# A linear-attention and two-layer-pair kernel: a third place for output copies, a shorter norm chain, ordered gram loads and new planner constants

## The chip, the cores and the metric

The kernel runs on one NeuronCore of a Trainium2 chip. The metric is the device time of one execution in microseconds (us); lower is better. TensorE (PE) has two clock levels, 1.2 and 2.4 GHz; the profile gives the granted share (0.5 or 1.0).

## The reference

```python
k_n = k / (norm(k) + 1e-6)                      # 4 batches x 8 heads, 768 tokens, 48 features
for t in range(768):                            # delta rule, state 48x48 per head
    y[t]   = q[t] @ state
    v_old  = state^T @ k_n[t]
    state += beta[t] * outer(k_n[t], v[t] - v_old)
x = y as [3072 tokens, 384]
x = elu(x @ w_in1) @ w_out1                     # first network, 384 -> 2048 -> 384
h = x @ w_in2                                   # second network
g = (a0 + a1 h + a2 h^2 + a3 h^3) / (1 + |b0||h| + |b1| h^2 + 1e-6)
out = g @ w_out2
```

## The kernel before, in words

**Numbers.** All is fp32. Each wide product is made of three fp32r matmuls on a high and a low part of both operands (high x high, high x low, low x high). The raw weights are taken apart bit by bit on the chip (`conv_load`, `conv_x`, `conv_d`, `conv_s`: a load of 192 KB, two ACT operations on it, one on DVE, and a split).

**Stages.** The 768 tokens are 12 subchunks of 64, two to a window, so there are 6 windows of 512 token columns. The attention of a window is: gram matrices of k with k and q (`g_item`, tile `gp`; 32 matmuls, which the trace shows as 64 MATMUL rows, because each plain fp32 matmul is two of them), the inversion of triangular matrices for all its heads (`t_pieces`, DVE with some ACT), then per subchunk the chain `ks`, `so` (tile `cb`), `lo`, `so`, `yy` (tile `y`), `xx` (transposes, tile `xt`) and `ku` in small matmuls. The first network of a window follows one window behind: for each of 16 blocks of hidden features nine matmuls into `h` (`H`), the elu on ACT and DVE (`A1`, `B1`, `C1`), nine matmuls into three accumulators `o` (`O`). After the 16 blocks `evac1` copies the three accumulators on ACT to tiles `xe` and stores each to `x2d` in DRAM. The second network reads `x2d` back and works on pairs of blocks (tiles `h_a`, `h_b`, `o`). "F" is the planner's name for the wide groups of nine matmuls.

**Order.** Nothing runs when it is recorded. `Recorder` collects all operations with their data dependences, and `order` plans them: `simulate` is a list scheduler on the host with a model of each engine, of the DMA bus and of instruction fetch for PE, and `backward` gives due times. It is run eight times, one run for each entry of `PUSH`; the plan with the earliest simulated end is the one that is emitted. Ties are moved by pseudo-random numbers (`draw`, `mixed`) whose seeds are in `MIX`. Any other seed or constant is therefore another order of the instructions on every engine's queue, of the DMA issues on SP too. Each queue runs in order.

**The planner's fetch model.** In `issue` and `stall` (lines 457 to 479) a counter adds up PE instructions, 2 for a matmul of the groups F and xx and 4 for others. The instructions come in blocks of some 254. A block is asked for when the counter gets within `room` of what is there, `wait` ns after that, at least `space` ns after the last request, and not before the modelled DMA bus is free; it can be used 2450 ns later. Where a small group would wait longer than `hold` for instructions, the planner takes a wide group first.

**Gram inputs.** `gin_ahead` loads k and q for the gram products, two halves (`hf` 0 and 1) of 512 KB for each subchunk. The first six halves have tiles of their own at the start; the other 18 go to two tiles `gin`. `g_item` asks for the next two halves at once, as soon as both tiles are free. `hold(t)` writes one element of a tile on POOL from another tile, so that the load into it waits for that. `follow`, in the change, uses the same means.

**Start.** `start` issues the first gram loads at once. Up to the first wide group PE has little to do; `gaps` puts unused matmuls (line 1501, tile `fill`, 512 columns each, two MATMUL rows per matmul) into the idle time that the plan shows.

**Norms.** For each window `pre1` gets the squared norms x of the keys and rr = x^-0.5 by Ln and Exp on ACT. `pre2` refines the norm on DVE (u = rr x, and a Newton step to t1), adds 1e-6, takes the reciprocal, squares it with a minus sign and multiplies with beta. The result scales the gram matrices before the inversion; t1, transposed to `n_t`, scales the values (`prep`, POOL).

Of the kernel before, what the change touches and what calls it, by code (L numbers as in the profile page):

```python
# [179 lines left out]
class Recorder:  # L180
# [129 lines left out]

PEC = {
    "F": (226.7, 425), "gp": (29, 475), "ks": (22, 330), "so": (22, 220), "lo": (22, 250), "yy": (31, 262), "ku": (47, 263),
    "xx": (90, 405), "wm": (200, 500), "yt": (33, 260)}
LEAVE = {"F": 2040, "so": 774, "lo": 812, "ks": 1500, "gp": 1086, "ku": 855, "yy": 1079, "xx": 290, "wm": 500, "yt": 1400}
ENTER = {"F": 0, "so": 71, "ks": 71, "xx": -25, "ku": 70, "yy": 20, "gp": 60, "lo": 100, "wm": 50, "yt": 20}
PAIR = {
# [3 lines left out]
SIZE = {"F": 9, "yy": 32, "yt": 48}  # L320
SLACK = {"small": 150, "F": 100, "x": 30, "issue": 450, "rate": 385, "land": 2300, "wait": 1500, "space": 3900, "room": 290, "first": 432, "hold": 400, "jit": 300,  "pj": 0}
MIX = [
    (44833516, 1), (87665163, 200), (70946401, 60), (44846256, 60), (55763056, 60),
]


PUSH = [(2000, 3000), (10000, 3000), (9000, 3000), (9000, 3000), (17000, 3000), (23000, 3000), (16000, 3000), (21000, 3000)]


def draw(seed, n):  # L330
# [71 lines left out]
def simulate(ops):  # L402
# [54 lines left out]
    def issue(u, t, k):  # L457
        nonlocal count, asked, shift
        shift = 0.0
        q = 2 if u.kind in ("F", "xx") else 4  # L460
        for o in u.ops:
            t0 = t + o.off * k + shift
            count += q
            if count > SLACK["first"] - SLACK["room"] + 254.6 * len(usable):
                asked = max(t0 + SLACK["wait"], asked + SLACK["space"], bus)
                usable.append(asked + 2450)
            if count > SLACK["first"] + 254.6 * used[0]:
                shift += max(0.0, usable[used[0]] - t0)
                t0 = max(t0, usable[used[0]])
                used[0] += 1  # L470
            o.start = t0

    def stall(u, t):
        n = len(u.ops) * (2 if u.kind in ("F", "xx") else 4)
        i = SLACK["first"] + 254.6 * used[0] - count
        if n < i:
            return 0.0
        a = usable[used[0]] if len(usable) > used[0] else max(t + SLACK["wait"], asked + SLACK["space"], bus) + 2450
        return a - t - max(0.0, i) / n * (u.ops[-1].off + u.ops[-1].pitch)

    def choose(e, t):
# [18 lines left out]
    while done < total:  # L500
        pick = None
        for e in free:
            if pend[e] or head[e]:
                t = free[e] if head[e] else max(free[e], pend[e][0][0])
                if pick is None or t < pick[0]:
                    pick = t, e
        t, e = pick
        while pend[e] and pend[e][0][0] <= t:
            _, n, u = heapq.heappop(pend[e])
            head[e].append((u.rank if e == "PE" else u.late, n, u))  # L510
        if e == "PE":
            small = [x for x in head[e] if x[2].kind != "F"] if mode not in (None, "F") else None
            x = min(small or head[e])
            if x[2].kind != "F" and SLACK["hold"] and stall(x[2], t) > SLACK["hold"]:
                wide = [y for y in head[e] if y[2].kind == "F"]
                if wide:
                    x = min(wide)
            head[e].remove(x)
            u = x[2]
            if mode is not None:  # L520
                stop = began + pe_cost(mode, u.kind) * size
                t = max(t, stop)
                clock(began, t if fill else stop, t)
                if fill and t > max(stop, 20000) + 500:
                    i = int((t - max(stop, 20000) - 300) / 430)
                    count += 4 * (i // 2 + i % 2)
                    while count > SLACK["first"] - SLACK["room"] + 254.6 * len(usable):
                        asked = max(t - 3000, asked + SLACK["space"], min(bus, t))
                        usable.append(asked + 2450)
                    while count > SLACK["first"] + 254.6 * used[0]:  # L530
                        used[0] += 1
            fill = fill and u.kind != "F"
            mode, began = u.kind, t
            k = 2.0 if slow else 1.0
            size = k * len(u.ops) / SIZE[mode] if mode in SIZE else k
            issue(u, t, k)
            began = t = t + shift
            free[e] = t + (u.ops[-1].off + u.ops[-1].pitch) * .95 * k
            for o in u.ops:
                finish(o, o.start + o.lat + 70 * (k - 1))  # L540
        else:
            o = choose(e, t)
            if o is None:
                free[e] = pend[e][0][0]
                continue
            o.start = t
            if e == "SP":
                if len(landed) >= 8:
                    t = o.start = max(t, landed[-8])
                free[e] = t + o.pitch  # L550
                bus = max(bus, t + 300) + o.bytes / SLACK["rate"]
                landed.append(max(t + o.lat, bus + SLACK["land"]))
                finish(o, landed[-1])
            else:
                if o.port:
                    t += max(0.0, port - t - 135)
                    port = t + o.lat
                free[e] = t + o.pitch
                finish(o, t + o.lat)
        done += 1  # L560
# [28 lines left out]
def kernel(  # L589
# [90 lines left out]
    def hold(t):  # L680
        gpsimd.tensor_copy(out=t[:, 0, 0:1], in_=gate[-1])

    conv_q = []
    for f in range(NF):
        conv_q += [("i1", f, h) for h in range(2)]
# [87 lines left out]
    def gin_ahead(n):  # L773
        for _ in range(n):
            i = gin_n[0]
            if i == len(gin_q) or i >= 4 and len(gate) < 2:
                return
            park = i < 6
            if park or gin_l[0] < 2:
                w, s, hf = gin_q[i]  # L780
                if park:
                    t = gin_park(i)
                else:
                    t = ap2.tile([128, 1024], F32, tag="gin", name="gin", bufs=2)
                    gin_l[0] += 1
                t = t.rearrange("p (u n) -> p u n", u=8)
                if 4 <= i < 8:
                    hold(t)
                rc.dma(out=t, in_=c_kg[s, hf])
                gin_t[s, hf] = t, not park  # L790
                gin_n[0] += 1
# [73 lines left out]
    def t_pieces(w):  # L865
# [17 lines left out]

        def pre2():
            v = vector
            x, rr, dg = st["x"], st["rr"], st["dg"]
            t1, u = small("t1"), small("nb")
            v.tensor_tensor(out=u, in0=rr, in1=x, op=ALU.mult)
            v.scalar_tensor_tensor(out=t1, in0=u, scalar=-0.5, in1=rr, op0=ALU.mult, op1=ALU.mult)
            v.scalar_tensor_tensor(out=t1, in0=t1, scalar=1.5, in1=u, op0=ALU.add, op1=ALU.mult)  # L890
            v.tensor_scalar(out=t1, in0=t1, scalar1=1e-6, scalar2=None, op0=ALU.add)
            v.reciprocal(out=rr, in_=t1)
            v.scalar_tensor_tensor(out=x, in0=rr, scalar=-1.0, in1=rr, op0=ALU.mult, op1=ALU.mult)
            v.tensor_tensor(out=x, in0=x, in1=bl_t.pop(w), op=ALU.mult)
            a = diag(am_f, 4)[:, :, :, 0:4]
            v.tensor_tensor(
                out=a, in0=a, in1=x.rearrange("p (d a) -> p d a", a=4).unsqueeze(3).to_broadcast([128, 8, 4, 4]), op=ALU.mult)
            v.tensor_scalar(
                out=tt_f[:, 0:132].rearrange("p (c x) -> p c x", x=33)[:, :, 0:32].rearrange("p c (b k) -> p c b k", k=4)[:, :, :, 0],
                in0=x.rearrange("p (b c) -> p c b", c=4), scalar1=-1.0, scalar2=None, op0=ALU.mult)  # L900
            for n in (4, 8):
                act(out=gs[n], in_=diag(am_f, 2 * n)[:, :, n:2 * n, 0:n], func=AF.Copy)
            gpsimd.memset(am[:, 0:16, 16:32], 0.0)
            n_t = ap2.tile([128, 32], F32, tag="n_t", name="n_t")
            n_d[w] = n_t
            v.transpose(out=n_t, in_=t1)
# [294 lines left out]
    def evac1(w):  # L1201
        NC = 256 * len(WINS[w])
        c0 = 256 * WINS[w][0]
        for c in range(3):
            if w == NW - 1:
                xs = p2q.tile([128, 512], F32, tag="ys", name="xe", bufs=3)[:, 0:NC]
            else:
                xs = mp.tile([128, 512], F32, tag="xe", name="xe")[:, 0:NC]
            act(out=xs, in_=acc[w][c][:, 0:NC], func=AF.Copy)
            rc.dma(out=x2d[:, c, c0:c0 + NC], in_=xs)  # L1210
        del acc[w]
# [141 lines left out]
            c += d  # L1353

    def start():
        gin_ahead(1)
        rc.dma(out=cm_sb, in_=mask_p)
        gin_ahead(3)
        load_beta(0)
# [227 lines left out]
```

## Time and profile before

| | |
|---|---|
| runs shown | 1003.8, 1006.26, 995.06 us; median 1003.8 |
| the profiled execution | 1006.48 us, span 1004.7 us |
| PE busy | 979.2 us, 97% |
| DVE, ACT, POOL busy | 819.8 us (82%), 692.6 us (69%), 311.7 us (31%) |
| share of the critical chain | PE 88%, DMA 4%, DVE 3%, ACT 2% |
| q1 data, q8 instruction packets | 59408 of 98.30 MB, 86 of 1.41 MB |

A busy PE is not a PE at its peak: matmuls overlap, and their ends are modelled. The chain of waits is followed back from the last instruction; "issue" in it is time in which an engine waited for nothing that the profile shows. In the rows, "[1.91 <-issue]" is idle time of the engine just before the instruction and what ended it.

### The profile page before, as it was taken

The page shows a single profiled execution, that of the slowest core. Times are in us where ns is not written, and L with a number is a line of the kernel's source. Part 1 is how long each engine was busy: PE and PEld are TensorE (multiplying, and loading weights), DVE is VectorE, ACT ScalarE, POOL GpSimd, SP SyncE. Part 2 cuts the span into 40 slices and gives each one's busy share as a digit, 9 for nine tenths or more (in the row PEclk, how much of TensorE's full clock was granted, in tenths as well). Part 3 has the DMA queues.
Part 4 walks back from the last instruction along what each step waited for, and adds up shares of the span by engine and source line. Part 5 has one row for each costly group of instructions (what it writes and reads, how often), then busy time and mean ns, then how long its engine had stood idle before and what let it go on. Part 6 is the DMA issues. An engine that isn't in the chain of part 4 may idle for free.

```text
span 1004.7 us, 26301 instructions
## 1 busy us (share of the span) xinstructions
PE 979.2 (97%) x11038; PEld 779.0 (78%) x11038; DVE 819.8 (82%) x1164; ACT 692.6 (69%) x1330; POOL 311.7 (31%) x218
## 2 busy tenths in 40 slices
PE   7989989999999999999999999999999999999997
PEld 4557777877787787788877888888888888888885
DVE  4998868956896996799543467999999999999997
ACT  4287878776867887686755577677676767766764
POOL 2000000432221231222112234363473644633341
PEclk9999999999999999999999999999999999999999
DMA  8352564146517543641505732001010010000000
GB/s 273 144 157 80 172 210 123 57 125 224 176 36 237 167 136 101 219 132 64 177 18 191 296 95 79 1 2 62 1 63 1 1 63 1 32 1 1 32 1 31
DMA packets 59526, 99.97 MB, mean 100 GB/s; under 512 B 6544, under 2 KB 39440, under 8 KB 59408
## 3 DMA queue, kind: packets, MB, share of 16 engines
q1 hardware_dynamic: 59408, 98.30, 30.1%
q8 instruction: 86, 1.41, 0.6%
q14 instruction: 32, 0.26, 0.1%
HBM read 76.25 MB, written 22.02 MB: 98 GB/s over the span
## 4 chain that ended last, share of the span: by engine, by line
PE 88%; DMA 4%; DVE 3%; ACT 2%; issue 2%; SPq 0%; ACTq 0%; DVEq 0%
PE o L198 37%; PE h L198 19%; PE h_b L198 10%; PE h_a L198 9%; PE cb L198 3%; PE fill L1501 3%; PE gp L198 2%; PE y L198 2%; PE ks L198 2%; DMA o2d<-cs 1%; PE ku L198 1%; DMA raw<-w_out 1%; DMA x2d<-xe 1%; PE h_c L198 1%; DVE wo L198 1%
## 5 line engine op out<-in xcount | busy, mean ns | idle before, releaser
L198 POOL TENSOR_TENSOR gl<-wo 128x1024 fp32r<-128x1024 f32 x47 | 145.8, 3103 | 200.2 <-DVE wo L198 134.5
L198 PE MATMUL o<-gh,wor 128*128 128x512 f32 x576 | 198.5, 401 | 1.9 <-ACT xe L198 1.9
L198 PE MATMUL h<-xh,wi 128*128 128x512 f32 x546 | 189.9, 405 | 0.0
L198 ACT ACTIVATE wo<-wo 128x1024 f32<-128x1024 f32 (+3 forms) x202 | 134.9, 698 | 59.5 <-DVE wo L198 54.2
L198 POOL TENSOR_TENSOR wor<-wo,wor 128x384 fp32r<-128x384 f32 x80 | 89.2, 1116 | 249.7 <-ACT wor L198 236.6
L198 PE MATMUL o<-gh,wo 128*128 128x512 f32 x576 | 138.5, 389 | 0.0
L198 PEld LDWEIGHTS o<-gh,wor 128*128 128x128 f32 x576 | 109.6, 190 | 27.1 <-ACT xe L198 2.3
L198 PEld LDWEIGHTS o<-gh,wo 128*128 128x128 f32 x576 | 108.1, 188 | 22.5
L198 PEld LDWEIGHTS h<-xh,wi 128*128 128x128 f32 x546 | 103.8, 190 | 24.5 <-issue 0.8
L198 PE MATMUL o<-gl,wor 128*128 128x512 f32 x288 | 113.7, 395 | 0.0
L198 DVE TENSOR_TENSOR gl<-e,gh 128x512 fp32r<-128x512 f32 x88 | 73.5, 835 | 42.3 <-ACT gh L198 40.4
L198 PE MATMUL h<-xl,wi 128*128 128x512 f32 x273 | 107.8, 395 | 0.0
L198 DVE SCALAR_TENSOR_TENSOR e<-e,h 128x512 f32<-128x512 f32 x91 | 62.1, 683 | 45.6 <-ACT e L198 45.2
L198 PE MATMUL h_b<-xh,wi 128*128 128x512 f32 x300 | 96.4, 389 | 0.0
L198 PE MATMUL h_a<-xh,wi 128*128 128x512 f32 x276 | 88.9, 389 | 0.0
L198 DVE SCALAR_TENSOR_TENSOR wo<-wo 128x1024 f32<-128x1024 f32 (+2 forms) x71 | 81.8, 1160 | 7.3 <-ACT wo L198 7.1
L198 ACT ACTIVATE e<-h 128x512 f32<-128x512 f32 x91 | 54.0, 593 | 48.4 <-PE h L198 48.1
L198 ACT ACTIVATE gh<-e 128x512 fp32r<-128x512 f32 x96 | 60.0, 625 | 25.9 <-DVE e L198 16.8
L198 PE MATMUL o<-gl,wo 128*128 128x512 f32 x288 | 73.5, 390 | 2.0 <-DVE gl L198 2.0
L198 DVE SCALAR_TENSOR_TENSOR gh<-wo,ab_sb 128x1024 fp32r<-128x1024 f32 (+1 forms) x49 | 63.6, 1297 | 8.8 <-ACT wo L198 3.2
L198 POOL TENSOR_TENSOR kv<-kv,n_t 128x384 f32<-128x384 f32 x24 | 23.1, 963 | 152.1 <-PE xt L198 67.0
L198 ACT ACTIVATE wo<-h_b,ab_sb 128x1024 f32<-128x1024 f32 (+1 forms) x52 | 57.0, 1127 | 18.2 <-PE h_b L198 18.2
(148 smaller groups left out, 1876.3 us busy)
## 6 DMA issues: line engine op xcount, KB each, us to landing
kq<-c_kq SPq DMA_DIRECT2D x22, 512.0 KB, 5.3
kv<-c_kv SPq DMA_DIRECT2D x24, 384.0 KB, 4.5
gin<-c_kg SPq DMA_DIRECT2D x18, 512.0 KB, 5.3
raw<-w_out SPq DMA_DIRECT2D x42, 192.0 KB, 3.5
raw<-w_in SPq DMA_DIRECT2D x34, 192.0 KB, 3.0
o2d<-cs SPq DMA_DIRECT2D x32, 192.0 KB, 3.4
i2d<-cs SPq DMA_DIRECT2D x32, 192.0 KB, 3.3
wi<-i2d SPq DMA_DIRECT2D x16, 384.0 KB, 3.5
```

What stands on the lines that cost most here:

```text
L198: fn(**{k: v.real() if isinstance(v, View) else v for k, v in kw.items()})
L1501: nc.tensor.matmul(out=wt["w"][:, 0:256 * n].rearrange("p (a b) -> p a b", a=n), lhsT=c[:, 128:256], rhs=c.unsqueeze(1).to_broadcast([128, ...
```

## The change

Besides other seeds and pushes for the planner, the model of instruction fetch gets other constants: blocks of 253.9 instead of 254.6, first 460 for 432, `room` 264 for 290, `wait` 900 for 1500, `space` 3500 for 3900 and 2250 for 2450 ns until a block can be used. A warm-up group "wm" of three matmuls of 512 columns stands ahead of the first loads, and its kind is counted with 2 instructions per matmul and costed at 585 ns each. `xe` gets three buffers in place of the pool's two. The second half of a gram pair from half 9 on (eight of the loads) waits by a one-element POOL copy for the landing of the first half. `pre2` takes 1/(x + 2e-6 u + 1e-12) straight away and makes t1 afterwards.

```diff
-    "xx": (90, 405), "wm": (200, 500), "yt": (33, 260)}
+    "xx": (90, 405), "wm": (585, 900), "yt": (33, 260)}
...
-SLACK = {... "wait": 1500, "space": 3900, "room": 290, "first": 432, "hold": 400, "jit": 300,  "pj": 0}
+SLACK = {... "wait": 900, "space": 3500, "room": 264, "first": 460, "blk": 253.9, "use": 2250, "hold": 400, "jit": 300,  "pj": 0}
 MIX = [
-    (44833516, 1), (87665163, 200), (70946401, 60), (44846256, 60), (55763056, 60),
+    (50701903, 1), (14530668, 200), (81070061, 60), (66735086, 60), (52417381, 200), (37322455, 600),
...
-PUSH = [(2000, 3000), (10000, 3000), (9000, 3000), (9000, 3000), (17000, 3000), (23000, 3000), (16000, 3000), (21000, 3000)]
+PUSH = [(1000, 0), (2000, 3000), (17000, 3000), (1000, 3000), (15000, 3000), (21000, 3000), (13000, 3000), (21000, 3000)]
...
-        q = 2 if u.kind in ("F", "xx") else 4
+        q = 2 if u.kind in ("F", "xx", "wm") else 4
...
+    def follow(t, u):
+        gpsimd.tensor_copy(out=t[:, 0, 0:1], in_=u[:, 0, 0:1])
...
                 if 4 <= i < 8:
                     hold(t)
+                elif i >= 8 and hf:
+                    follow(t, gin_t[s, 0][0])
                 rc.dma(out=t, in_=c_kg[s, hf])
...
+            v.tensor_scalar(out=t1, in0=x, scalar1=1e-12, scalar2=None, op0=ALU.add)
             v.tensor_tensor(out=u, in0=rr, in1=x, op=ALU.mult)
+            v.scalar_tensor_tensor(out=x, in0=u, scalar=2e-6, in1=t1, op0=ALU.mult, op1=ALU.add)
+            v.reciprocal(out=x, in_=x)
+            v.scalar_tensor_tensor(out=x, in0=x, scalar=-1.0, in1=bl_t.pop(w), op0=ALU.mult, op1=ALU.mult)
             v.scalar_tensor_tensor(out=t1, in0=u, scalar=-0.5, in1=rr, op0=ALU.mult, op1=ALU.mult)
             v.scalar_tensor_tensor(out=t1, in0=t1, scalar=1.5, in1=u, op0=ALU.add, op1=ALU.mult)
             v.tensor_scalar(out=t1, in0=t1, scalar1=1e-6, scalar2=None, op0=ALU.add)
-            v.reciprocal(out=rr, in_=t1)
-            v.scalar_tensor_tensor(out=x, in0=rr, scalar=-1.0, in1=rr, op0=ALU.mult, op1=ALU.mult)
-            v.tensor_tensor(out=x, in0=x, in1=bl_t.pop(w), op=ALU.mult)
...
-                xs = mp.tile([128, 512], F32, tag="xe", name="xe")[:, 0:NC]
+                xs = mp.tile([128, 512], F32, tag="xe", name="xe", bufs=3)[:, 0:NC]
...
     def start():
+        z = tmp[:, 0:512]
+        vector.memset(z, 0.0)
+        rc.brk("wm")
+        for _ in range(3):
+            mm(out=h_s[0], lhsT=z[:, 0:128], rhs=z, start=True, stop=True)
         gin_ahead(1)
```

## Rows read from the trace of the kernel before

**Rows 1.** Busy us by stage: PE, PEld, DVE, ACT, POOL, clock, DMA share, GB/s

```profile
50.00:81.00 31.00, 26.09 (x857) 17.34 (x854) 27.83 (x74) 27.99 (x87) 1.97 (x3) 1.00 0.56 172
81.00:550.00 469.00, 461.13 (x7575) 367.79 (x7576) 351.76 (x690) 341.51 (x848) 103.42 (x96) 0.99 0.43 136
600.00:977.00 377.00, 377.00 (x1665) 312.28 (x1664) 353.60 (x274) 260.52 (x266) 177.91 (x77) 1.00 0.07 24
```

**Rows 2.** PE's waits from 81 to 620 us: total, times, longest

```profile
PE ks L198 <- issue: 3.0, 1, 3.0
PE ks L198 <- ACT gl__2915 L198: 2.4, 1, 2.4
PE gp L198 <- issue: 1.9, 1, 1.9
PE o L198 <- ACT xe L198: 1.9, 1, 1.9
```

**Rows 3.** Chain of waits from 78 to 95 us: start, length, what

```profile
79.09 1.91 issue
...
81.44 5.93 PE h L198 x18
...
88.86 2.26 PE h L198 x9
```

**Rows 4.** Chain of waits from 135 to 150 us

```profile
139.24 2.95 issue
...
142.52 3.11 PE h L198 x9
145.63 2.79 PE o L198 x9
```

**Rows 5.** DMA from 134 to 143 us: issues, KB, us to landing

```profile
gin<-c_kg SPq DMA_DIRECT2D x2, 512.0 KB, 8.1
```

**Rows 6.** Timeline from 235 to 248 us, all engines

```profile
236.55 1.19 SPq L198 DMA_DIRECT2D gin<-c_kg  x2
...
240.69 0.36 ACT L198 ACTIVATE cs<-ce 128x192 fp32r<-128x192 f32 x1 [0.83 <-DMA o2d<-cs]
...
241.37 2.04 PE L198 MATMUL ks<-s_st,kq 48*32 48x48 f32 x128 [2.35 <-ACT gl__2915 L198]
```

**Rows 7.** Chain of waits from 236 to 252 us

```profile
243.42 3.53 PE o L198 x9
```

**Rows 8.** Chain of waits from 540 to 560 us

```profile
538.50 8.84 DMA x2d<-xe
...
549.26 3.28 PE o L198 x8
552.53 2.48 PE h L198 x9
```

**Rows 9.** The stretch after 549.9 us, columns as in rows 1

```profile
549.90:553.20 3.30, 3.30 (x10) 2.52 (x9) 1.83 (x3) 2.46 (x6) 1.01 (x1) 0.50 1.03 400
```

**Rows 10.** Chain of waits from the start

```profile
5.88 1.74 PE gp L198 x54
...
9.57 2.81 PE gp L198 x95
...
12.78 1.22 PE gp L198 x33
...
26.20 1.09 PE gp L198 x64
```

**Rows 11.** Weight loads of the unused matmuls, 12 to 20 us

```profile
15.80 0.33 PEld L1501 LDWEIGHTS fill<-cm_sb 128*128 128x128 f32 x1 [0.52 <-issue]
16.65 0.33 PEld L1501 LDWEIGHTS fill<-cm_sb 128*128 128x128 f32 x1 [0.52 <-issue]
```

**Rows 12.** The norm chain's DVE operations: duration ns min/median/max

```profile
L198 DVE SCALAR_TENSOR_TENSOR t<-nb,rr x6: 183/191/193, 19.0 to 423.8; 128x32 f32<-128x32 f32 x6
```

**Rows 13.** Packets of the fetch queue from 470.9 to 474.4 us

```profile
q8 instruction: 2, 0.03, 3.6%
```

More of the change, by code (lines that the diff above doesn't have):

```diff
@@ L312 @@
     "F": (226.7, 425), "gp": (29, 475), "ks": (22, 330), "so": (22, 220), "lo": (22, 250), "yy": (31, 262), "ku": (47, 263),
-    "xx": (90, 405), "wm": (200, 500), "yt": (33, 260)}
-LEAVE = {"F": 2040, "so": 774, "lo": 812, "ks": 1500, "gp": 1086, "ku": 855, "yy": 1079, "xx": 290, "wm": 500, "yt": 1400}
+    "xx": (90, 405), "wm": (585, 900), "yt": (33, 260)}
+LEAVE = {"F": 2040, "so": 774, "lo": 812, "ks": 1500, "gp": 1086, "ku": 855, "yy": 1079, "xx": 290, "wm": 1755, "yt": 1400}
 ENTER = {"F": 0, "so": 71, "ks": 71, "xx": -25, "ku": 70, "yy": 20, "gp": 60, "lo": 100, "wm": 50, "yt": 20}
@@ L320 @@
 SIZE = {"F": 9, "yy": 32, "yt": 48}
-SLACK = {"small": 150, "F": 100, "x": 30, "issue": 450, "rate": 385, "land": 2300, "wait": 1500, "space": 3900, "room": 290, "first": 432, "hold": 400, "jit": 300,  "pj": 0}
+SLACK = {"small": 150, "F": 100, "x": 30, "issue": 450, "rate": 385, "land": 2300, "wait": 900, "space": 3500, "room": 264, "first": 460, "blk": 253.9, "use": 2250, "hold": 400, "jit": 300,  "pj": 0}
 MIX = [
-    (44833516, 1), (87665163, 200), (70946401, 60), (44846256, 60), (55763056, 60),
+    (50701903, 1), (14530668, 200), (81070061, 60), (66735086, 60), (52417381, 200), (37322455, 600),
+    (39513789, 60), (96818129, 600), (44511796, 200), (58732419, 200), (61486538, 200), (56621892, 200),
+    (59016650, 200), (65322403, 200),
 ]
-PUSH = [(2000, 3000), (10000, 3000), (9000, 3000), (9000, 3000), (17000, 3000), (23000, 3000), (16000, 3000), (21000, 3000)]
+PUSH = [(1000, 0), (2000, 3000), (17000, 3000), (1000, 3000), (15000, 3000), (21000, 3000), (13000, 3000), (21000, 3000)]
 def draw(seed, n):
@@ L463, in issue @@
             count += q
-            if count > SLACK["first"] - SLACK["room"] + 254.6 * len(usable):
+            if count > SLACK["first"] - SLACK["room"] + SLACK["blk"] * len(usable):
                 asked = max(t0 + SLACK["wait"], asked + SLACK["space"], bus)
-                usable.append(asked + 2450)
-            if count > SLACK["first"] + 254.6 * used[0]:
+                usable.append(asked + SLACK["use"])
+            if count > SLACK["first"] + SLACK["blk"] * used[0]:
                 shift += max(0.0, usable[used[0]] - t0)
@@ L473, in stall @@
     def stall(u, t):
-        n = len(u.ops) * (2 if u.kind in ("F", "xx") else 4)
-        i = SLACK["first"] + 254.6 * used[0] - count
+        n = len(u.ops) * (2 if u.kind in ("F", "xx", "wm") else 4)
+        i = SLACK["first"] + SLACK["blk"] * used[0] - count
         if n < i:
             return 0.0
-        a = usable[used[0]] if len(usable) > used[0] else max(t + SLACK["wait"], asked + SLACK["space"], bus) + 2450
+        a = usable[used[0]] if len(usable) > used[0] else max(t + SLACK["wait"], asked + SLACK["space"], bus) + SLACK["use"]
         return a - t - max(0.0, i) / n * (u.ops[-1].off + u.ops[-1].pitch)
@@ L526, in simulate @@
                     count += 4 * (i // 2 + i % 2)
-                    while count > SLACK["first"] - SLACK["room"] + 254.6 * len(usable):
+                    while count > SLACK["first"] - SLACK["room"] + SLACK["blk"] * len(usable):
                         asked = max(t - 3000, asked + SLACK["space"], min(bus, t))
-                        usable.append(asked + 2450)
-                    while count > SLACK["first"] + 254.6 * used[0]:
+                        usable.append(asked + SLACK["use"])
+                    while count > SLACK["first"] + SLACK["blk"] * used[0]:
                         used[0] += 1
@@ L885, in pre2 @@
             v = vector
-            x, rr, dg = st["x"], st["rr"], st["dg"]
+            x, rr = st["x"], st["rr"]
             t1, u = small("t1"), small("nb")
+            v.tensor_scalar(out=t1, in0=x, scalar1=1e-12, scalar2=None, op0=ALU.add)
             v.tensor_tensor(out=u, in0=rr, in1=x, op=ALU.mult)
+            v.scalar_tensor_tensor(out=x, in0=u, scalar=2e-6, in1=t1, op0=ALU.mult, op1=ALU.add)
+            v.reciprocal(out=x, in_=x)
+            v.scalar_tensor_tensor(out=x, in0=x, scalar=-1.0, in1=bl_t.pop(w), op0=ALU.mult, op1=ALU.mult)
             v.scalar_tensor_tensor(out=t1, in0=u, scalar=-0.5, in1=rr, op0=ALU.mult, op1=ALU.mult)
```

## The prediction, made before the change had run

> **What bounds the kernel now.** I read the busy times by stage first, then PE's waits, then the chain of waits around each of them, and last the start. By stage [rows 1] PE is the bound from the first wide group to the end: it is busy 461 of 469 us between 81 and 550 us, and all of the 377 us between 600 and 977 us, where 1665 matmuls take 0.226 us each, or 2.04 us for a wide group of nine. The change leaves that second part as it is, and takes no matmul out of the first; so what can be won there is only PE's waits and what follows them. Ahead of 81 us it is DVE and ACT that are full (27.8 and 28.0 of 31 us [rows 1]), and PE fills time with unused matmuls.
>
> PE waits four times for long between 81 and 620 us [rows 2]; the reader is to see in the chains that each wait costs twice. After each one PE runs for some 3.3 us at 1.2 GHz: the granted clock is 0.50 in such a stretch [rows 9]. The price shows in the wide groups, which take 2.26 us after small matmuls and 2.04 after another wide group [rows 3]:
> - C, at 79 us: 1.91 us of "issue", then 18 matmuls in 5.93 in place of 2.26 + 2.04: 1.63 more [rows 3]. Together 3.5.
> - B, at 139 us: 2.95 of "issue" in the middle of a `ks` group, then 3.11 + 2.79 in place of 4.30: 1.60 more [rows 4]. Together 4.5.
> - D, at 239 us: 2.35 for ACT's copy of gram results [rows 6], then 3.53 in place of 2.26: 1.27 more [rows 7]. Together 3.6.
> - A, at 546 us: 1.9 for `xe` [rows 2], then 17 matmuls in 5.76 in place of 3.85: 1.9 more [rows 8]. Together 3.8.
> These four are 15.4 us, 3.9 each. The sum below is made against the profiled execution, 1006.5 us (span 1004.7, 1.8 around it). It is 2.7 above the median of the runs shown, and these spread over 11 us: I read that as some executions having fewer of these waits than the profiled one, and therefore don't shift the sum by the 2.7.
>
> **The change part by part.**
>
> *Three places for `xe`.* The third copy of a window waits until the store of the first has left its place, and that store took 8.84 us at 538 us, among weight loads [rows 8]. A third place takes the wait away, with its slow stretch: **-3.8**. Of five windows with `xe` one paid, so this is all there is; the low end is 0, if the new order puts the stores elsewhere. It only costs memory.
>
> *Gram inputs one after the other.* The pair issued at 135 us needed 8.1 us to land [rows 5], and B lies just behind it; the pair at 236.55 us is followed by ACT waiting for another transfer and by D [rows 6]. With `follow`, only 512 KB stand ahead of another transfer, the 16 KB blocks of instructions among them. Cost: eight POOL copies of one element, off the path. The second load is later by a landing, up to 8.1 us [rows 5], but waits on SP, where the loads of weights, k, q and v, and the stores, queue behind it; their readers are ACT and POOL. That is covered as long as the plan puts the issue behind the landing; if not, the price is a D, 3.6 us. I take B whole and D half: **-4.5 and -1.8**; ends 0 and -8.1.
>
> *New fetch constants, seeds and pushes.* The constants let the planner believe in a fetch that is asked for 600 ns earlier, can follow another after 3.5 instead of 3.9 us and is usable 200 ns sooner. The trace bears one of them out: two fetches lie in 3.5 us [rows 13]. C is of this kind, with no gram pair ahead of it. I take half of it, **-1.8**; the ends are 0 and -3.5. All orders are new, and so is where small groups stand; a new wait of the usual size is likely somewhere among 7575 matmuls [rows 1]: **+3.9**, with ends 0 and four such, +15.6.
> The page "Runtime: NRT & Kernel Launch" of the Trainium skill, section "Instruction fetch mechanics", speaks against any gain here: it has instructions come in blocks of 16 KiB and their crossing mostly hidden. By it alone B and C would not be fetches, and the sum would be 6.3 us higher. The trace differs in that PE stops for 2.95 us within one group whose inputs are there.
>
> *Warm-up matmuls.* The gram products at the start run slowly: 95 rows in 2.81 us and 33 in 1.22 [rows 10], 30 to 37 ns each, against 64 in 1.09 (17 ns) at 26 us. The unused matmuls behind them begin 0.85 us apart [rows 11], twice the 0.43 that 512 columns take later, so PE is at 1.2 GHz up to there. Three matmuls of 512 columns are six rows; at that level 6 x 0.85 = 5.1 us, from about 1.3 us (an estimate for the DVE memset, DVE being idle) to 6.4, where the first gram products begin in earnest at 5.88: a loss of 0.5 if the clock stays low. If it rises, the last 128 rows, which start at 9.57 and end at 14.00, take 2 x 1.09 = 2.2 plus some stop for instructions: a gain of at most 2.2. I take **-1.3**, nearer to the gain, because PE then enters the gram products from dense work. What follows is DVE's inversion, full up to 81 us, so the gain is passed on.
>
> *Norm chain.* From rr to the factor it was seven DVE operations and becomes four (x + 1e-12 can be made while ACT makes rr): three of some 0.19 us [rows 12], **-0.6** once, on the first window's path; the other windows have a whole window's time. DVE does one operation more per window, 6 x 0.19 = 1.1 us, covered where it is busy 352 of 469 us [rows 1]. Without that cover, +0.2 a window.
>
> **Sum:** 1006.5 - 3.8 - 4.5 - 1.8 - 1.8 + 3.9 - 1.3 - 0.6 = 996.6; I say **996**.
>
> **Rivals.**
> - *Clean.* No new wait, B, C and D all gone: 1006.5 - 15.4 - 1.9 = **989**. For it: all four have causes that the change addresses, and 995 among the runs shows that fewer waits do happen. Against: every order is new, and waits are found only when the plan meets the chip.
> - *Waits come back.* The "issue" waits don't hang on the gram pairs or the constants, and as many lie in other places: only `xe` and the start remain, 1006.5 - 3.8 - 1.9 = 1001, or 1005 with one more: **1002**. For it: C without a gram pair, and the spread of the runs. This is also what the page named above would lead to.
> - *Slower: the fetch model is too hopeful.* With 600 ns less until a request and 200 less until use, the planner keeps small groups (2 matmul rows and 2 weight loads per matmul) together that it used to part by wide ones; PE runs dry inside them, as in B. Place: the runs of `gp`, `ks`, `yy` between 81 and 550 us. Price 3.9 each, on top of 1001: from the first extra one it is slower than the median shown, from the fourth (1016) by more than 1%. Against: rows 13.
> - *It doesn't do what it says:* the clock stays low through the start and the warm-up delays the gram products by 0.5 instead; then the forecast is 998.5. This is inside the range of the forecast.
>
> **How the numbers follow.** About 1% (10 us) is what a measurement of this kernel can tell from no change; the bounds are 993.8 and 1013.8. Forecast, 0.40: 996, its own range 992 to 1000. Clean, 0.25: 987 to 992. Waits come back, 0.22: 1000 to 1006. Slower, 0.13: 1005 to 1020. The range from 988 to 1007 leaves out some 0.07 below and 0.11 above. Faster by over 1%: nearly all of clean and a third of the forecast, 0.38. Slower by over 1%: most of the fourth, 0.10. Within: 0.52.
>
> **What would show it.** In the profile after: no wait of ACT `xe` for the store, and no 0.50 clock stretch at the last window's change (A); gram loads issued one by one, several us apart, and no "issue" wait of PE over 1 us in the 10 us behind them (B); ACT's waits for `raw` and `cs` behind gram loads shorter (D); the first 64-row gram groups nearer 1.1 than 1.8 us each, and the first wide `h` group before 80 us instead of 81.4 (warm-up, norm); the stretch from 600 to 977 us still 0.226 us per matmul. The prediction is wrong if the first wide group comes later than 81.4, if the small matmuls and switches between 81 and 550 take another sum than before by more than the waits, or if there are more than two 0.50 stretches.

## The result and the profile after

The changed kernel takes 992.6 us in the median of 20 runs, the kernel before 1004.0 in the 20 beside them: the ratio is 0.9904, with a 95% interval of 0.988 to 0.9929. The range of 988 to 1007 holds it, and it is 3.4 us below the 996 forecast. One of the 20 runs after took 5465 us; the median and the ratio do not hang on it, and nothing on record says what it was. The profiled execution after took 990.7 us (span 988.9) against 1006.5 (1004.7), 15.8 us less.

By stage (busy us and number of instructions of PE, PEld, DVE, ACT and POOL, then granted clock, DMA share and GB/s), the two stretches of [rows 1] in which PE is the bound:

```profile
81.00:550.00 469.00, 468.05 (x7621) 374.62 (x7620) 363.19 (x702) 353.99 (x869) 106.24 (x107) 1.00 0.46 147
600.00:977.00 377.00, 377.00 (x1664) 312.15 (x1664) 359.71 (x279) 261.56 (x265) 175.93 (x72) 1.00 0.06 22
```

PE was idle for 7.9 of the 469 us before and is for 0.95 now. The second stretch is what it was, 0.226 us per matmul. PE's waits from 81 to 620 us, all that the trace names, against [rows 2]:

```profile
PE gp L198 <- DMA gin<-c_kg: 0.7, 2, 0.4
PE ks L198 <- issue: 0.3, 1, 0.3
```

All four long ones are gone, and one of a new kind is there: gram products waiting for their own loads. The chain of waits (start, length, what) at the first wide group and at the `ks` group of [rows 4]:

```profile
78.97 0.86 issue
79.84 0.45 PE gp L198 x15
80.29 4.29 PE h L198 x18
...
137.38 1.26 PE ks L198 x105
138.64 0.28 issue
138.92 0.46 PE ks L198 x23
139.37 2.28 PE o L198 x9
```

C is down from 1.91 to 0.86 us of issue and B from 2.95 to 0.28, and neither is followed by slow wide groups: 18 in 4.29 us where [rows 3] have 5.93.

Where the 15.8 us come from is read by setting the starts of the same wide matmul side by side, counted from the first in both traces. The first begins 1.15 us earlier (80.22 against 81.37); by the 288th the lead is 8.1 us (C's slow stretch and B), by the 720th 12.3 (D among others), and it falls back to 10.5 at the 1440th, since small groups stand elsewhere. By the 1584th it is 14.6 (A), and stays so to the last pair; the end adds 1.2. That last piece was not in the sum. In it PE waits for DVE's last `gl`, 1.97 us before and 0.95 after. DVE's operations stand in the same order there, but one of them takes longer before (start, length, operation; before, then after):

```profile
991.05 1.52 DVE L198 SCALAR_TENSOR_TENSOR wo<-wo 128x512 f32<-128x512 f32 x1
...
997.07 0.96 PE L198 MATMUL o<-gl,wo 128*128 128x512 f32 x3 [1.97 <-DVE gl L198]
```

```profile
976.10 0.69 DVE L198 SCALAR_TENSOR_TENSOR wo<-wo 128x512 f32<-128x512 f32 x1
```

No run shows why.

### The profile page after: what moved, and what is told of

Its sections match the earlier page's. It is cut to its first block, busy times and chain, and to the rows that moved or that the text cites. A ratio compares the mean times of both kernels' runs of the same rounds, so it can differ in the third digit from the quotient of the medians.

```text
span 988.9 us, 26297 instructions
## 1 busy us (share of the span) xinstructions
PE 973.8 (98%) x11042; PEld 774.0 (78%) x11042; DVE 822.5 (83%) x1171; ACT 695.8 (70%) x1330; POOL 309.2 (31%) x226
## 4 chain that ended last, share of the span: by engine, by line
PE 91%; DMA 4%; DVE 2%; issue 1%; ACT 1%; POOL 0%; SPq 0%; ACTq 0%; POOLq 0%; DVEq 0%
PE o L198 38%; PE h L198 20%; PE h_b L198 10%; PE h_a L198 9%; PE cb L198 3%; PE gp L198 2%; PE y L198 2%; DMA gin<-c_kg 2%; PE ku L198 2%; PE fill L1514 2%; PE ks L198 2%; PE h_c L198 1%; PE xt L198 1%; DMA wo<-w_in 1%; DMA xg<-c_kg 1%
## 5 line engine op out<-in xcount | busy, mean ns | idle before, releaser
L198 PE MATMUL o<-gh,wor 128*128 128x512 f32 x576 | 196.1, 396 | 0.0
L198 DVE TENSOR_TENSOR gl<-e,gh 128x512 fp32r<-128x512 f32 x88 | 71.3, 810 | 33.4 <-ACT gh L198 31.9
L198 ACT ACTIVATE wor<-wo 128x384 fp32r<-128x384 f32 x96 | 49.8, 518 | 24.4 <-PE o L198 23.9
```

The source lines that it names most:

```text
L198: fn(**{k: v.real() if isinstance(v, View) else v for k, v in kw.items()})
```

## The experiments

A change of one constant gives another order of everything. So most kernels below keep an order that was planned, before's or after's, and take a part in or out at the moment of emission ("its own order"); three are planned anew and said to be. Ratios are to the kernel before, run on the same chip at the same time (its median was between 1000.9 and 1005.1 us).

**The third place, in the order of before.**

```diff
-            self.obj = self.pool.real.tile(self.shape, self.dt, **self.kw)
+            kw = dict(self.kw, bufs=3) if self.kw.get("tag") == "xe" else self.kw
+            self.obj = self.pool.real.tile(self.shape, self.dt, **kw)
```

> The kernel before with three places for xe and nothing else: every queue keeps its order of before. Theory (each part removes the wait that it names): the 3.3 us wait of ACT for the store at 546 us, PE's 1.9 us behind it and the half-clock stretch go, and the end comes 3.8 us earlier than in the same order with two places, so about 1000 us against 1004. Rival (the order decides, the parts are worth nothing by themselves): the wait goes but the time stays within 1 us of before, since another wait takes its place.

Ratio 0.9959 (0.9929 to 0.9989), 4.1 us less. PE's waits in its profile from 81 to 620 us:

```profile
PE ks L199 <- issue: 3.3, 1, 3.3
PE ks L199 <- ACT gl__2915 L199: 2.2, 1, 2.2
...
```

B and D are as before and A is gone: between the 1440th and the 1584th wide matmul this execution gains 4.1 us on the one before. The theory holds, with the size forecast. The start shows how much an order varies by itself. With the order of before the first wide group begins at 83.3 us here and at 81.4 in the profile before, and C is 0.5 us of issue without its slow stretch, though nothing in this kernel addresses it. (It has a wait of 2.3 us for issue at 62.5 us, which the profile before has not.)

**Two places, in the order of after.** The edit is the same with `bufs=2`, and each store of `xe` is moved right behind its copy on SP's queue.

> The changed kernel with two places for xe in the order that was planned for three; only the stores of xe are put right behind their copies on SP's queue, since two places need that. Theory (the third place is worth 3.8 us): a wait of ACT for a store of xe comes back in at least one of the five windows, with a PE wait near 2 us and a half-clock stretch: 996 against 992.6. Rival (the order has made the third place idle): no PE wait over 1 us behind xe, and the time within 1 us of 992.6.

Ratio 0.999 (0.9962 to 1.0018), median 1003.5 us: nearly the whole gain is lost. In its profile, who waited for `xe` (total, times):

```profile
  ACT xe L200: 12.6, 5
  PEld o L200: 3.8, 1
  PE o L200: 3.3, 1
```

ACT now waits in five places, where before it did once, 3.3 us. At the last window PE waits 3.3 us, and 6.8 us at half clock follow; that place alone costs 6.3 us there (between the 1440th and the 1584th wide matmul). The rest of what the profile lost, 6.0 us, lies in other waits of 0.7 to 1.5 us, of which some come in other kernels too; the moved stores can have a part in them. So the third place is worth more in an order that was planned for it than in the old one: theory right, size too small.

**The gram pair together again, in the order of after.** The copies are left out, and the second load stands right behind the first.

```diff
+    for o in plan:
+        if o.mark == "follow" or o in second.values():
+            continue
+        first.append(o)
+        if o.mark and o.mark[0] == "gin":
+            first.append(second[o.mark[1]])
```

> The changed kernel in its own order without the one-element copies, and with the second half of each gram pair from pair 4 on issued right behind the first on SP, as it was before the change. Theory (two 512 KB loads in a row hold up the instruction blocks and the loads behind them): waits of PE for issue or for ACT of 2 to 3 us, each with a half-clock stretch, come back behind two of the seven later pairs, 8 us together: about 1000. Rival (the waits went because the new order puts fewer small groups behind a pair): no PE wait over 1 us behind any pair, 992.6 within 1 us.

Ratio 0.9951 (0.9918 to 0.9984); medians 998.3 against 992.6, but the intervals overlap with those of the changed kernel. PE's waits from 81 to 620 us in its profiled execution, which took 993.7 us:

```profile
PE ks L199 <- ACT gl__5930 L199: 1.5, 1, 1.5
PE ks L199 <- ACT gl__3069 L199: 1.1, 1, 1.1
...
```

These are of the kind of D, and no issue wait is over 0.3 us: B did not come back in this execution. But it is the fourth shortest of twelve. Seven took 998 to 1005 us, five of them with a mean granted clock of 0.990 or 0.991, as against 0.997 in the profiled one, so PE ran longer at half clock in them, and no trace says where. The median is nearer to the theory's 1000 than to the rival's 992.6. For D the theory is borne out in small; for B it is open. What the ordering is worth here is somewhere between nothing and 6 us.

**No warm-up, in the order of after.** The memset and the three matmuls are not emitted.

```diff
+    first = [o for o in first if o.mark != "wm"]
```

> The changed kernel in its own order without the DVE memset and the three warm-up matmuls. The profile of the changed kernel has its first wide group at 80.2 us against 81.4 before, and the small gram group ahead of it begins at 78.09 us in both. Theory (the start is bound by DVE and ACT behind the gram products, and loses the gain again): gram products at half clock again, 30 to 37 ns a row, later by 1 to 2 us, but the first wide group within 0.5 us of 80.2 and the time within 1 us of 992.6. Rival (the gain of 1.3 us forecast for the warm-up is passed on): the first wide group 1.3 us later and about 994.

Ratio 0.9911 (0.9876 to 0.9946), no difference from the changed kernel that these runs can tell. The first wide group begins at 77.6 us, earlier than with the warm-up, which neither theory nor rival had. The chain shows B, though, with one gram load of 512 KB ahead of it, not two:

```profile
134.55 1.34 PE ks L199 x111
135.90 3.45 issue
139.35 0.60 PE ks L199 x17
139.95 4.14 PE o L199 x9
```

**Is it the twelve instructions?** Small matmuls in place of the dense ones keep the count of instructions; 32 more of them move each block by half (`count` is 1, 1, 1 in the first kernel, and 1, 1, 33 in the second, as it is popped).

```diff
+            if o.mark and o.mark[0] == "wm":
+                z, n = o.mark[1], count.pop()
+                for _ in range(n):
+                    nc.tensor.matmul(out=h_s[0][0:32, 0:128].real(), lhsT=z[0:48, 0:32].real(), rhs=z[0:48, 0:128].real(), start=True, stop=True)
```

> The changed kernel in its own order, with the three warm-up matmuls cut from 512 columns to 128 and from 128 x 128 to 48 x 32 weights: as many PE instructions as in the changed kernel, but no dense work. The kernel without the warm-up had PE waits of 3.45 us at 136 us and 1.97 at 330 that the changed kernel does not have. Theory (the plan rests on where the instruction blocks end, and taking 12 instructions out moved them): those waits go again, and the time is 991 to 993. Rival (the dense warm-up itself keeps these waits away, or they come and go by chance): a PE wait over 1.5 us in a ks or gp group, 996 or more.

Ratio 0.9921 (0.9891 to 0.9952), median 992.5, no wait over 0.6 us between 81 and 620 us. By itself this spoke for the theory, but for one issue wait of 1.8 us in a `ks` group at 60 us, which the changed kernel's second profile has too.

> As the kernel with the small warm-up matmuls, and 32 more of them, in a stretch in which PE waits for its first load anyway: 128 PE instructions more, so every later block of instructions ends half a block earlier in the plan's order. Theory (the fetch model's constants earn their time by where blocks end): PE waits of 2 to 3.5 us in small groups come back, three or more, 8 to 12 us: 1000 to 1004. Rival (the place of the blocks does not matter; waits are made by DMA load alone): 991 to 994, as with three small ones.

Ratio 1.0038 (1.0007 to 1.007). But the start was spoilt by the added matmuls themselves: they all write the same place, and 69 rows took 14.92 us, 0.216 us each; the first wide group came at 88.8 us, 8.6 late. Its time lies in the theory's range for that reason alone. Behind the start no PE wait is over 1.7 us, so the waits of 2 to 3.5 us did not come either. The same with outputs in 16 different places (64 columns each):

> As the kernel with 32 more small matmuls, but these go to changing places of the accumulator in place of one, where each took 0.216 us and made the start 8.6 us later. Again 128 PE instructions more than planned. Theory (the place of the blocks matters): the first wide group within 2 us of 80.2, and PE waits over 1.5 us in small groups at two or more places behind it, 996 to 1000. Rival (it does not matter): 991 to 994.

Ratio 0.9913 (0.988 to 0.9947), first wide group at 80.21 us, median 995.4 beside 995.8 of the changed kernel on that chip. No issue wait over 0.2 us behind 81 us; its 3.1 us of waiting is for gram loads. The theory falls: the gain does not hang on where blocks end to within half a block. (One gram wait of 1.9 us is the size that the theory named, but it is for data.)

**The old seeds, planned anew.** `MIX` and `PUSH` of before, the rest of after.

> The changed kernel with the MIX and PUSH of before, so planned anew with the new fetch constants and all other edits. Theory (third place, ordered gram loads and constants carry the gain, any seeds will do): within 3 us of 992.6. Rival (the gain is in the order that these seeds found): PE waits over 1.5 us in two or more places of the first network, 998 or more.

Ratio 0.995 (0.9917 to 0.9982). Two PE waits, 2.2 us for a gram load and 1.9 of issue, and 1.99 at the tail. The time is within 3 us of 992.6, as the theory has it, though the two waits are as the rival has them. Half to two thirds of the gain is there without the new seeds (0.5% of 0.74 to 0.96%); 1.0 us of what they add is the tail.

**The old constants, planned anew.** `SLACK`, `PEC`, `LEAVE` and the count of before, the rest of after.

> The changed kernel with the planner's constants of before (fetch model, warm-up cost and count) and its new seeds, so planned anew. Theory (the fetch constants let the plan part small groups where blocks end late): PE waits for issue of 2 to 3 us come back in two or more places, 998 to 1003. Rival (the constants are worth nothing): within 3 us of the kernel with new constants and the seeds of before.

Ratio 0.9991 (0.9959 to 1.0023). PE waits 2.0 us for issue in a `ks` group, 0.9 for DVE, 0.7 for a gram load, 1.94 at the tail, and runs at half clock for 6.8 us ahead of the first wide group. The time is as the theory says, its cause only in part: one wait of the kind forecast, not two.

**The new constants alone, planned anew.** The kernel before with after's `SLACK`.

> The kernel before with the new fetch constants only, its own seeds and pushes, and so planned anew; two places for xe. Theory (the constants part small groups where blocks come late): no PE wait for issue over 1 us between 81 and 550 us, the wait for xe stays: 0.992 to 0.996 of before. Rival (constants without the other parts are one more random order): waits of 2 to 3 us in other places, 0.998 to 1.004 of before.

Ratio 0.9977 (0.9952 to 1.0002). A and D don't appear in its profile, though `xe` has two places as before: the wait for it was forecast to stay. So A hangs on the order too. B is larger than ever:

```profile
PE ks L198 <- issue: 4.8, 1, 4.8
PE cb L198 <- issue: 0.8, 1, 0.8
```

**Third place and gram copies, in the order of before.** As the first kernel, with the copy emitted ahead of each second load.

```diff
+            if o.mark:
+                t, u = o.mark
+                nc.gpsimd.tensor_copy(out=t[:, 0, 0:1].real(), in_=u[:, 0, 0:1].real())
             o.emit()
```

> The kernel before in its own order with the third place for xe and with the one-element copies, put on POOL right ahead of the second load of each gram pair, so not planned for. The third place alone gave 0.9959 of before. Theory (ordered gram loads take away the waits at 139 and 239 us, whatever the order): neither wait over 1 us, and 6 to 8 us less than with the third place alone, 992 to 995 against 1004. Rival (those waits belong to the order of the small groups, and SP and POOL now stand still for a landing eight times): the waits stay or move by some 10 us, 1000 to 1008.

Ratio 1.0039 (1.0009 to 1.0069): the copies cost 0.8% on top of the third place, instead of giving as much. PE's waits from 81 to 620 us, and what SP waited for the copies:

```profile
PE gp L200 <- DMA gin<-c_kg: 3.1, 3, 1.4
PE ks L200 <- issue: 2.7, 1, 2.7
PE cb L200 <- ACT R L200: 2.0, 1, 2.0
PE gp L200 <- issue: 1.5, 1, 1.5
...
SPq L200 <- POOL gin L1510: 36.3, 8, 5.6
```

SP's wait in the changed kernel, whose planner knew of the copies (9.7 us in its second profile):

```profile
SPq L198 <- POOL gin L198: 9.1, 6, 3.4
```

B stays (2.7 us), C is there (the 1.5 us of issue), D shrinks to 0.6, and four new waits come, three for gram loads and one for `R`. The one for `R`, 2.0 us, is ACT standing 4.48 us for a weight load that SP issued late: it stands behind the gram pair on SP's queue, whose two issues take from 328.98 to 335.59 us.

**The changed kernel again.**

> The changed kernel itself once more, beside these on the same chip. Theory: no PE wait over 1 us between 81 and 550 us in this profile either, 0.988 to 0.993 of before. Rival (its first profile was a lucky execution): one or two waits of 2 to 3 us.

Ratio 0.9926 (0.9888 to 0.9964). Its profiled execution took 996.6 us and has a wait that the first did not, again for a gram load, with a slow stretch behind it (`h`, nine in 2.74 us):

```profile
307.68 7.29 DMA gin<-c_kg
314.97 0.14 issue
315.11 1.53 PE gp L198 x59
316.63 1.45 PE ku L198 x32
318.08 2.74 PE h L198 x9
```

The rival is right: the first profile was a lucky execution, and this one has one such wait. Here the first wide group begins at 81.24 us, as late as before the change (81.37).

## Why the prediction was right, step by step

- **What bounds the kernel: right.** The time moved by PE's waits and their slow stretches, and by 1.2 us at the end, which the sum did not have. Wide groups, switches and the stretch from 600 to 977 us are as before.
- **A, -3.8: right.** 4.1 us in the order of before, in ratio and trace alike. Missed was that the planner uses the place: with two, five copies wait in the new order. And a third place is not the only way: with the new constants alone no PE wait for `xe` came with two.
- **B, -4.5 for the ordered gram loads: the size came, the reason is not shown.** B is 0.28 us in the first profile after. But it stays with the ordering in the old order (2.7 us) and comes once in the new (3.45), so the ordering by itself does not take it away. Without the ordering it is not in the one profile there is, of one of the shorter executions (pair together again); the longer ones have no trace. What the packets show is that B is a late block of instructions. Data from one block to the next, before (131.5 to 139.7 us), then the late block itself (139.7 to 142.2; queue: packets, MB, share of the DMA engines):

```profile
q1 hardware_dynamic: 1184, 2.37, 89.5%
...
q8 instruction: 1, 0.02, 2.3%
```

  The block's packet runs from 139.93 to 140.85 us, and PE goes on at 142.19, 1.34 us behind it. The lag is much the same wherever PE waits over 1 us for issue in a small group: 1.53 us in C, 1.38 behind the wait of 4.8 us, 1.38 without the warm-up. So C is a late block too. The same two in the changed kernel, 131.5 to 136.4 and 136.4 to 139:

```profile
q1 hardware_dynamic: 746, 1.50, 87.0%
...
q8 instruction: 1, 0.02, 2.4%
```

  And in the kernel with the new constants alone, whose wait was 4.8 us, from 130.8 to 141.3, when its block came:

```profile
q1 hardware_dynamic: 1483, 3.21, 89.7%
```

  Where PE hardly waits, the block comes after 1.5 MB of data, and where it waits long after 2.4 to 3.2 MB (2.5 without the warm-up, with one gram load among them). These amounts show less than they seem to: the data ran at 289 to 322 GB/s in each, so they say only how long ago the block before had come (some 5 us, or 8 to 10.5). One case does not fit: with both parts in the old order PE waits 2.7 us, and the block came after 1.6 MB.

  A rival is that PE asked for these blocks late, and not that data held them up. PE's instructions, counted in the traces, speak against it. After 600 us, where little data moves, a block starts with every 255 to 256 of them. Carried back from there, less 15 of them, this gives a count at which a block can have been asked for (an estimate; it puts the blocks after 600 us some 1.6 us behind their count). B's block starts 5.1 us after PE has reached its count, and 5.5 without the warm-up, against 2.3 for the same block in the changed kernel. In the profile before, from 60 us on, none of 37 blocks is more than 3 us behind its count where the DMA engines are under 10% busy in the microsecond after, and 12 of 24 are where they are over 60% busy (3 of 31 in the first profile after). So blocks come late where the DMA engines are busy. That the second half of a gram pair does it is only argued. Moving the blocks by half of one brought no such wait back.
- **D, -1.8: the direction right.** 2.35 us before, 0.6 with the copies in the old order, 1.1 and 1.5 in the new one without them.
- **The price of `follow`: its covered part was too simple.** I named weights, k, q, v and stores as what queues behind the wait on SP, and left out the gram products themselves. Half of the pairs are read 9 to 12 us after they are asked for (loads at 301.2 and 305.9 us, products at 311 in the first profile), so the later second half can be late: 0.7 us in one profile, 2.3 in the other. The condition given, that the plan must put the issue behind the landing, is what decides: SP stood 36 us where it did not and 9 where it did.
- **C, -1.8, and the constants: the size came, the reason is not shown.** Issue at the first wide group fell by 1.05 us and the slow stretch behind it went. But the same happened in the order of before with the third place alone, where C is 0.5 us, so C comes and goes by itself. Constants alone are worth 0.2%, unclear; taken out of the change they cost about 0.7 to 0.9%. So they seem to pay together with the order planned by them; each of these kernels is one order, though, and no run shows the fetch model as the reason.
- **Warm-up, -1.3: wrong.** The clock does rise early: to 1.0 at 7.6 us, against 17.4 before and 9.3 without the warm-up in its own order; in the second profile of the changed kernel it is back at 0.5 from 11.9 to 18.7. The chain has six rows of the warm-up from 1.45 us, 5.49 us long, and the first 64 gram rows in 1.42 us where [rows 10] pay 1.74 for 54. But DVE's transposition of the gram matrices begins at 14.0 and 15.6 us in the two profiles of the changed kernel, at 15.2 without the warm-up, at 15.3 with the small one, and at 15.9 before: the kernel without it lies between the two profiles with it. The warm-up itself holds PE up to 6.94 us, and the last products still stop 0.5 us for instructions.
- **Norm chain, -0.6: the chain is shorter, by more than forecast.** From the start of ACT's Exp to the scaling of the gram matrices it takes 1.40 us instead of 2.66, in the first window. Before and after, DVE's operations on x (start, length):

```profile
18.76 0.19 DVE L198 TENSOR_TENSOR nb<-rr,x 128x32 f32<-128x32 f32 x1
...
20.28 0.77 DVE L198 TENSOR_TENSOR x<-x,bl 128x32 f32<-128x32 f32 x1
21.16 0.78 DVE L198 TENSOR_TENSOR am<-am,x 128x128 f32<-128x128 f32 x1
```

```profile
18.64 0.19 DVE L198 TENSOR_TENSOR nb<-rr,x 128x32 f32<-128x32 f32 x1 [1.88 <-ACT rr L198]
18.87 0.19 DVE L198 SCALAR_TENSOR_TENSOR x<-nb,t 128x32 f32<-128x32 f32 x1
19.09 0.35 DVE L198 RECIPROCAL x<-x 128x32 f32<-128x32 f32 x1
19.48 0.19 DVE L198 SCALAR_TENSOR_TENSOR x<-x,bl 128x32 f32<-128x32 f32 x1
19.78 0.29 DVE L198 TENSOR_TENSOR am<-am,x 128x128 f32<-128x128 f32 x1
```

  The three operations saved are 0.6; the other 0.6 is the multiplication with beta, which took 0.77 us here before and 0.19 after. Over the six windows before it takes 0.19 to 0.98 us, though another tensor-tensor of this size (`nb`) always takes 0.19; no run shows why. I took 0.19 for all and had not read that row. No run tested the chain by itself, so what it adds to the time is not shown.
- **The start as a whole, -1.9: not delivered.** The first `ks` begins 1.1 us earlier (60.2 against 61.3), yet the gram products at 78.09 us begin at the same time in both first profiles: the chain after runs through two loads of `wo` from `w_in`, 4.85 and 4.51 us long. Only C's share is left of it. The first wide group, forecast before 80 us, begins at 80.2 and 81.2 in the two profiles, and in three profiles of the order of before at 81.3, 81.4 and 83.3.
- **New waits, +3.9: none in the first profile, about one in the second.** This is most of the difference between clean (989, which the first profile met within 2 us) and the forecast; the median lies between them.
- **Slower, the fetch model too hopeful: no.** The change has fewer issue waits, not more. The kernel with the new constants alone has 4.8 us in one `ks` group, so it could happen.
- **The rule that crossings are mostly hidden** (the Trainium skill, "Runtime: NRT & Kernel Launch", "Instruction fetch mechanics"), by which B would be no fetch: the trace disagrees here. PE's wait of 2.95 us ends 1.34 us behind the block that the fetch queue brings.
- **The sum as a whole: partly luck.** A is shown. B and C came with their sizes but without the reasons given, the 1.9 us of the start did not come, the 1.2 us at the end were not foreseen, and the 3.9 us for new waits was too much for the first profile. That these nearly cancel, 3.4 us from the forecast, is luck.

## What to carry to other kernels

Where one engine is the bound all along, count its waits and what each leaves behind it in a slow stretch: here each of the four cost 3.5 to 4.5 us, a third to a half of it after the wait was over. A part that makes a transfer wait must be known to whatever sets the order of the queues; the same eight copies cost 0.8% in an order planned without them. And a single profile of a kernel whose waits come and go shows one draw: two profiles of the same program differed by 6 us.

## What the runs showed of the hardware that was not expected

- 69 small matmul rows that write one and the same place in the accumulator took 0.216 us each. Spread over 16 places (with 64 columns instead of 128, so two things changed) they took 0.055, and the start cost nothing: the first wide group came at 80.21 us instead of 88.8.
- Behind some PE waits the stretch at half clock was longer than the 3.4 us behind each of the four before. Without the warm-up it was 6.8 us: after the 3.45 us, nine wide matmuls took 4.14 us and 64 rows of `cb` behind them 1.44, where 2.28 and 0.81 are usual. Behind the 3.3 us for `xe` it was 6.8 us too.
- The granted clock rose to 1.0 at 7.6 us with the warm-up and at 9.3 without it in the same order, and the time of the two kernels does not differ by what these runs can tell.
- Where PE waited over 1 us for issue in a small group, between 40 and 560 us, it went on 1.2 to 1.6 us behind the end of a packet of the fetch queue, in each of the twelve profiles that have such a wait.
